# Attention and gated mixing on one core: P times V wholly in float16 passes from pair ten, relu in place in PSUM, row sums turned before their reciprocal

## The chip, the core and the metric

The kernel runs on one NeuronCore of a Trainium2 chip. The core has a matmul engine (TensorE, PE in the profile, with PEld for its weight loads), VectorE (DVE), ScalarE (ACT), GpSimd (POOL) and SyncE (SP), which here issues the DMAs. The metric is the time of one execution on the device in microseconds (us). Three runs of the kernel before gave 939.5, 941.02 and 941.13, median 941.02. A change of less than about 0.2% cannot be told from none.

## The reference

Eight batches, twelve heads, 448 positions, head size 64; everything is float32 at the input and the output.

```python
def rmsnorm(x, g):
    return x / np.sqrt(np.mean(x * x, axis=-1, keepdims=True) + 1e-06) * g
scores = np.matmul(rmsnorm(q, g_q), rmsnorm(k, g_k).transpose(0, 1, 3, 2)) / np.sqrt(64)
attn = np.exp(scores - scores.max(-1, keepdims=True))
attn = attn / (attn.sum(-1, keepdims=True) + 1e-09)
x = np.matmul(attn, v)            # then heads side by side: (8, 448, 768)
h = np.maximum(x @ w_in, 0.0)     # w_in (768, 1024)
# conv: three taps along the sequence, zero at the ends, weights conv_w (3, 1024)
conv = conv_w[0] * h_previous + conv_w[1] * h + conv_w[2] * h_next
out = (h * sigmoid(conv)) @ w_out # w_out (1024, 768)
```

## The kernel before

**Tiles and stages.** Two heads make a pair; there are 48 pairs, six to a batch. A pair's 896 query rows are cut into seven tiles of 128. For a pair the kernel loads q, k and v, squares and sums q and k (L365, L371), forms the inverse root with small steps on the tile `st` (L393 to L408), scales (`apply_rms`), turns k and q into `kT` and `qT`, and multiplies them into seven score tiles (`scores`, L606 and L615). For each tile DVE takes the row maximum (`soft_max`, L619), and ACT forms exp and its row sum (`soft_exp`, L627). The seven sums of a row stand in `rsum`, 128x7.

To multiply P with V, P has to be turned. In pairs 0 to 9 PE turns all seven tiles in float32 (`p_transpose`, L657), ACT or DVE copies them out of PSUM (`p_evac`, tile `PT`), and `pv` (L732) multiplies in float32. In pairs 10 to 47 the first four of the seven tiles take another way: they are split into a float16 high part (`p_hi`) and a float16 rest (`p_lo`), and both are turned by a transposing DMA (`p_turn`, on SP's queue). The other three go on as before. So `pv` has two parts there: 16 instructions in float32 for the 192 columns of each head from the three tiles (L732), and 24 in float16 (L741) for the 256 columns from the four, in three passes: high by high, high by rest of v, rest by high. Both heads' results lie in one PSUM tile, 64 partitions each. For this v is scaled in place by a power of two (`v_scaled`, L705, POOL or DVE), and split into `vp` (`v_hi` on ACT, POOL or DVE; `v_lo` on POOL or DVE).

**Row sums.** `sum_step` adds 1e-9 to `rsum` (L672) and takes the reciprocal (L674), both on DVE; PE turns it to 7x128 (`sum_transpose`, L677, the tile `t_('r'_n`), it is copied out as `rT`, written to memory and read back broadcast over 64 partitions as `rB`. `x_scale` (L748) multiplies pv's result by it, and x is split into two float16 halves.

**The second half.** When a batch has its six pairs, the input stage multiplies x with `w_in` in eight units `fc` of 128 channels, 18 float16 matmuls each (`in_part`, L814, tile `m_('i'_batch_fc`). ACT applies relu out of PSUM into one of two buffers `hbuf` (L824). The middle tap is a scaled copy (`in_conv` 0, L101 on ACT or L103 on DVE), the two outer taps are multiply-adds on DVE (L835), then come tanh on ACT (L841), the gate on DVE (L845), and the split of the gated result into float16 halves (`in_hi`, `in_lo`, L97 and L109). The output stage multiplies these with `w_out` (`out_part`, L884, 24 or more matmuls a tile), copies the result out and stores it.

**Buffers.** PSUM has eight tiles: ring `s` of three for scores, ring `t` of two for transposes, and ring `m` of three, which `pv`, `in_part` and `out_part` share in the order in which they begin. A ring's next tile waits until the tile that many places before has been read for the last time.

**Order of the work.** All steps go into a plan. Each has a due time, from the pair's `base`, offsets in `PH`, and a shift for its name in `SHIFT`; `needs` lists what it waits for, `options` the engines that can do it with a cost, and `PH` an added patience for an engine other than the first. A planner then simulates the engines and writes out one fixed order for each, so that an instruction that waits holds back all that stand behind it on its engine. `SHARED` and `LOCKS` name the steps that, in the planner's model, may not run at the same time on DVE and POOL.

`copy` (L97), `copy_scaled` (L101, L103) and `binary` (L109) are helpers, so many steps share these lines.

Of the kernel before, what the change touches and what calls it, by code (L numbers as in the profile page):

```python
# [19 lines left out]
PH = dict(  # L20
    T=17.282, ti=32.607, si=4.103, so=7.453, hop=0.682, beta=0.029, wi0=-44.74, wi1=135.29,
    wo0=37.16, wo1=179.858, cw=28.289, p_evac=1.569, p_hi=3.998, p_lo=0.384, p_rms=0.085,
    p_v=1.807, p_x=2.279, p_g=2.547, p_relu=3.044, p_cv=0.644, p_qz=2.756, p_ev=0.549, sp=0.066,
    nbulk=3, p_rs=0.015, p_sq=2.22, p_w=4.641, v0=10.619, dg=2, n1=10, q1=10, nf=10, pvs=4,
    p_vs=2.149, p_qh=16.119, p_ql=3.843, p_ph=0.609, p_pl=1.368,
)
PACE = [
    17.594, 18.751, 18.399, 19.788, 14.185, 15.143, 10.221, 13.443, 24.304, 18.98, 20.544,
    19.525,
]  # L30
SHIFT = dict(
    prepare=-39.537, load_g=220.765, make_g=44.125, load_cw=-40.223, make_cw=-61.71,
    load=26.853, convert=189.422, bound=32.819, bound_max=140.72, bound_turn=45.662,
    bound_row=85.601, bound_spread=2.83, scale=25.643, in_factor=265.161, split=128.634,
    rest=-7.056, out_factor=196.209, load_k=256.594, load_q=-7.691, square=166.921,
    square_sum=130.145, rsqrt=76.729, apply_rms=170.731, qk_transpose=55.459, qk_hi=52.477,
    q_middle=-2.488, v_load=240.331, v_bound=-11.069, scores=90.947, soft_max=-2.101,
    soft_exp=75.799, p_transpose=169.491, p_evac=1.057, sum_step=101.401, sum_transpose=184.031,
    sum_evac=42.518, sum_store=11.342, sum_load=0.212, v_scaled=-2.289, pv=113.916,
    x_scale=34.057, x_hi=47.234, x_lo=4.93, v_max=-22.175, v_turn=247.886, v_row=47.937,  # L40
    v_spread=-7.616, v_scale=10.402, qk_lo=-3.699, q_hi=-1.114, q_lo=32.611, q_turn=32.138,
    p_hi=277.959, p_lo=-8.271, p_turn=158.327, v_hi=22.662, v_lo=19.094, moe_scales=-30.954,
    in_part=39.441, in_relu=250.285, in_conv=-0.625, in_tanh=167.33, in_gate=-2.024,
    in_hi=21.395, in_lo=7.763, in_carry=2.204, out_scales=155.356, out_part=185.578,
    out_evac=47.388, out_store=8.134,
# [23 lines left out]
def tile_attention_moe(ctx: ExitStack, tc, q, k, v, g_q, g_k, w_in, conv_w, w_out, out):  # L69
# [41 lines left out]
    def move(e, dst, src):  # L111
# [14 lines left out]
        rB=2, vacc=2, vsc=4, cwb=3, s=3, t=2, m=3, rd=2, rsum=2, rT=2, mx=10, h=2, ph=3, vp=2,  # L126
# [40 lines left out]
    hbuf = [const.tile([P, S + 2], F32, name=f"hbuf{i}") for i in range(BUFS["h"])]  # L167
# [414 lines left out]
    def places(n):  # L582

        if ("PT", n) not in rings.setdefault("PT", Ring(BUFS["PT"])).d:
            new("PT", n, [P, NB * NS * P], F32)
        t, w = old("PT", n), NB * (NS - nd(n)) * P
        return (
            t[:PB, :w].rearrange("p (k q) -> p k q", k=NB),
            t[:, w:].bitcast(F16).rearrange("p (a k q) -> p a k q", a=2, k=NB) if nd(n) else None,
        )  # L590
# [56 lines left out]
    def p_turn(n, j):  # L647
        c = SLOTS[j] if SLOTS[j] < 3 else SLOTS[j] + nd(n) - NS
        nc.sync.dma_start_transpose(
            places(n)[1].rearrange("p a k q -> p (a k) q")[:, :, c * P : (c + 1) * P],  # L650
            old("ph", (n, j)).rearrange("q a k p -> q (a k p)"),
        )
# [7 lines left out]

    def p_evac(n, j):
        c = SLOTS[j] - nd(n) // 2
        copy(
            on["p_evac", n, j], places(n)[0][:, :, c * P : (c + 1) * P],
            old("t", ("p", n, j))[:PB].rearrange("p (k q) -> p k q", k=NB),
        )

    def sum_step(n, i):

        r = old("rsum", n)  # L670
        if i == 0:
            nc.vector.tensor_scalar(r, r, 1e-9, None, op0=ALU.add)  # L672
        else:
            nc.vector.reciprocal(r, r)  # L674
# [6 lines left out]
    def sum_evac(n):  # L681
        copy(on["sum_evac", n], new("rT", n, [NS, P], F32), old("t", ("r", n))[:NS, :P])
# [14 lines left out]
    PV_STEP = PH["pvs"]  # L697
    PV3 = ((0, 0), (0, 1), (1, 0))

    def pvs(n):  # L700
        return (*range(0, NB, PV_STEP), *(range(NB, NB + 3) if nd(n) else ()))
# [14 lines left out]
    def heads(n, k0):  # L716

        wd = nd(n) // 2 * P
        wt = S - wd
        if k0 < NB:  # L720
            return (slice(wd, S), slice(0, wt)), (slice(0, wt), slice(wt, 2 * wt))
        return (slice(0, wd), slice(wt, S)), (slice(0, wd), slice(wd, 2 * wd))

    def pv(n, k0):
        if k0 == 0:
            new("m", ("v", n), [P, 512], F32, psM)
        ps, (out, col) = old("m", ("v", n)), heads(n, k0)
        if k0 < NB:
            v, pt = old("v", n), places(n)[0]
            for k in range(k0, k0 + PV_STEP):  # L730
                for h in range(2):
                    nc.tensor.matmul(  # L732
                        ps[HALF[h], out[h]], v[:, h, k], pt[:, k, col[h]],
# [802 lines left out]
```

## Time and profile before

| | us |
|---|---|
| median of three runs | 941.02 |
| the profiled execution | 939.03 |
| its span, first to last instruction | 937.2 |
| PE busy | 876.9 |
| DVE busy | 747.5 |
| ACT busy | 678.7 |
| POOL busy | 633.9 |

The profile is one execution, recorded by the hardware. "Busy" counts the time in which an engine had an instruction under way; matmuls overlap, so a busy PE need not be at its peak. Windows give busy time by engine in a stretch of the span. The chain that ended last is followed back from the last instruction, at each step to whatever released it. A wait is put down to the releaser that came last. Names of tiles carry the pair or the batch, so `m_('v'_23_5636` is the result of `pv` of pair 23, and a row like `PE t_('r'_14 ... <- DVE rsum` is the transpose of pair 14's sums waiting for DVE. The span falls into a first part of some 180 us with attention alone and the preparing of the weights, a middle in which attention of one batch runs between the input and output stages of an earlier one, and a tail from about 872 us on with only the last batch's input and output stage.

### The profile page before, as it was taken

The page shows a single profiled execution, that of the slowest core. Times are in us where ns is not written, and L with a number is a line of the kernel's source. Part 1 is how long each engine was busy: PE and PEld are TensorE (multiplying, and loading weights), DVE is VectorE, ACT ScalarE, POOL GpSimd, SP SyncE. Part 2 cuts the span into 40 slices and gives each one's busy share as a digit, 9 for nine tenths or more (in the row PEclk, how much of TensorE's full clock was granted, in tenths as well). Part 3 has the DMA queues.
Part 4 walks back from the last instruction along what each step waited for, and adds up shares of the span by engine and source line. Part 5 has one row for each costly group of instructions (what it writes and reads, how often), then busy time and mean ns, then how long its engine had stood idle before and what let it go on. Part 6 is the DMA issues. An engine that isn't in the chain of part 4 may idle for free.

```text
span 937.2 us, 18350 instructions
## 1 busy us (share of the span) xinstructions
PE 876.9 (94%) x6352; PEld 502.8 (54%) x6352; DVE 747.5 (80%) x1308; ACT 678.7 (72%) x1571; POOL 633.9 (68%) x702
## 2 busy tenths in 40 slices
PE   3788899899998999989998999989998999999998
PEld 1344445446654656555655656555654565556555
DVE  6889988898899777897899777897898966991540
ACT  3778879787787876787788876787786877784331
POOL 3483673887888776786877776786877876682120
PEclk9999989999999999999999999999998999999999
DMA  8764452147866768557866679457865777355001
GB/s 195 189 178 131 120 146 66 31 103 162 168 131 122 142 148 174 89 120 153 179 126 119 139 148 185 93 115 152 182 123 91 134 160 135 71 96 116 17 17 51
DMA packets 286572, 117.60 MB, mean 125 GB/s; under 512 B 247744, under 2 KB 282896, under 8 KB 286480
## 3 DMA queue, kind: packets, MB, share of 16 engines
q1 hardware_dynamic: 286480, 116.44, 59.3%
q8 instruction: 50, 0.82, 0.4%
q14 instruction: 42, 0.34, 0.1%
HBM read 56.65 MB, written 11.18 MB: 72 GB/s over the span
## 4 chain that ended last, share of the span: by engine, by line
PE 71%; DVE 19%; ACT 4%; POOL 3%; issue 2%; DMA 1%; SPq 0%; ACTq 0%; DVEq 0%; POOLq 0%
DVE st L371 1%; DVE rsum L672 1%; DVE vacc L534 1%; DVE c_(6_3_10681 L835 1%; DVE wo L216 1%; DVE wo L307 1%; DVE rB L748 1%; PE m_('v'_5_1272 L732 1%; DVE c_(2_4_4782 L835 1%; DVE wi L307 1%; DVE wo L224 1%; PE m_('i'_5_6_9284 L814 1%; DVE carry L860 0%; PE m_('o'_1_0_0_3560 L884 0%; PE m_('o'_5_0_0_9557 L884 0%
## 5 line engine op out<-in xcount | busy, mean ns | idle before, releaser
L814 PEld LDWEIGHTS <-wi 128*128 128x128 f16 x1152 | 113.0, 99 | 97.7 <-issue 7.3
L884 PEld LDWEIGHTS <-gring 128*128 128x128 f16 (+1 forms) x1056 | 102.2, 99 | 58.4 <-issue 5.6
L109 POOL TENSOR_TENSOR sq<-qkf,st 112x512 f32<-112x512 f32 x77 | 88.2, 1159 | 10.6 <-DVE st L393 8.6
L705 POOL TENSOR_SCALAR v<-v,vsc 112x512 f32<-112x512 f32 x37 | 63.1, 1711 | 24.3 <-DVE vsc L206 13.5
L109 POOL TENSOR_TENSOR x<-rB,x 128x448 f16<-128x448 f32 x45 | 49.4, 1098 | 33.2 <-ACT x L97 32.7
L371 DVE TENSOR_REDUCE st<-sq 112x16 f32<-112x1024 f32 x48 | 58.0, 1209 | 6.0 <-ACT sq L365 6.0
L741 PEld LDWEIGHTS <-vp 112*64 112x64 f16 x912 | 49.0, 110 | 7.5 <-issue 4.5
L615 PEld LDWEIGHTS <-qT 64*128 64x128 f16 x684 | 24.3, 94 | 44.8 <-issue 33.7
L365 ACT ACTIVATE sq<-qkf 112x1024 f32<-112x1024 f32 x42 | 44.3, 1056 | 5.0 <-DMA qkf<-in_q_dram 5.0
L109 POOL TENSOR_TENSOR qkf<-sq,qkf 112x512 f16<-112x512 f32 x37 | 46.2, 1249 | 2.2 <-ACT qkf L97 1.9
L109 POOL TENSOR_TENSOR vp<-v,vp 112x512 f16<-112x512 f32 x29 | 35.7, 1232 | 3.1 <-ACT vp L97 1.5
L97 ACT CAST x<-rB 128x448 f16<-128x448 f32 x47 | 26.4, 561 | 11.0 <-DVE rB L748 10.8
L498 POOL COPY qz<-qT 64x128 f16<-64x128 f16 x76 | 31.6, 415 | 3.7 <-DMA qT<-qkf 1.4
L534 DVE TENSOR_REDUCE vacc<-v 112x1 f32<-112x512 f32 x48 | 32.3, 672 | 1.1 <-DMA v<-in_v_dram 0.7
L97 ACT CAST qkf<-sq 112x512 f16<-112x512 f32 x38 | 23.4, 618 | 10.3 <-POOL sq L109 10.3
L672 DVE TENSOR_SCALAR rsum<-rsum 128x7 f32<-128x7 f32 x48 | 27.3, 570 | 3.9 <-ACT e_(47_6_11318 L627 3.4
L884 PEld LDWEIGHTS <-carry 128*64 128x64 f16 x192 | 19.2, 109 | 10.6 <-issue 4.5
L884 PEld LDWEIGHTS <-wi 128*128 128x128 f16 (+1 forms) x192 | 19.4, 101 | 9.7 <-ACT wi L97 0.7
L399 POOL TENSOR_SCALAR st<-st 112x32 f32<-112x32 f32 (+1 forms) x15 | 5.3, 355 | 24.0 <-DVE st L371 23.3
L860 DVE COPY carry<-gring 128x128 f16<-128x128 f16 x32 | 15.1, 472 | 5.7 <-POOL gring L109 5.7
L109 DVE TENSOR_TENSOR sq<-qkf,st 112x512 f32<-112x512 f32 x19 | 18.1, 954 | 1.0 <-POOL st L396 0.9
L494 POOL COPY qz<-qT 64x64 f32<-64x64 f32 x20 | 9.0, 449 | 13.6 <-ACT qT L97 11.4
(3642 smaller groups left out, 3068.7 us busy)
## 6 DMA issues: line engine op xcount, KB each, us to landing
qkf<-in_k_dram SPq DMA_DIRECT2D x48, 224.0 KB
qkf<-in_q_dram SPq DMA_DIRECT2D x48, 224.0 KB
v<-in_v_dram SPq DMA_DIRECT2D x48, 224.0 KB
rB<-rd SPq DMA_DIRECT2D x96, 112.0 KB
wo<-in_moe_w_in_dram SPq DMA_DIRECT2D x12, 512.0 KB
gring<-in_moe_w_out_dram SPq DMA_DIRECT2D x16, 384.0 KB
PT<-ph SPq DMA_TRANSPOSE x152
rd<-rT SPq DMA_DIRECT2D x48, 3.5 KB
```

Of the source, the lines that this page charges most:

```text
L97: (nc.scalar.copy if e == "ACT" else elementwise(e).tensor_copy)(dst, src)
L109: elementwise(e).tensor_tensor(dst, a, b, op=op)
L365: nc.scalar.activation(sq, old("qkf", n), AF.Square)
L371: nc.vector.tensor_reduce(old("st", m)[:, 0, n - m].rearrange("p i s -> p (i s)"), old("sq", n).rearrange("p i h t d -> p (i h t) d"), axi ...
L498: e.tensor_copy(z[HALF[h], :, HALF[h]], old("qT", n)[HALF[h], :, t0 : t0 + 64])
L534: nc.vector.tensor_reduce(old("vacc", b)[:PB, i : i + 1], old("v", n).rearrange("p h t d -> p (h t d)"), axis=AX.X, op=ALU.max, apply_abso ...
L615: nc.tensor.matmul(ps[u][:, :S], lhs, kt[r, w], start=(i == 0), stop=(i == 2))
L672: nc.vector.tensor_scalar(r, r, 1e-9, None, op0=ALU.add)
L705: elementwise(on["v_scaled", n]).tensor_scalar(v, v, old("vsc", n // NP)[:PB, 1:2], None, op0=ALU.mult)
L741: nc.tensor.matmul(ps[HALF[h], out[h]], v[:, w, h, k], pt[:PB, a, k, col[h]], start=(i == 0 and k == 0), stop=(i == 2 and k == NB - 1),)
L814: nc.tensor.matmul(ps[:, :S], wi[:, wl, c, fc * P : (fc + 1) * P], old("x", b * NP + c)[:, xl], start=(i == 0), stop=(i == 3 * NP - 1),)
L884: nc.tensor.matmul(ps[p0 : p0 + m, :NO2], g, wo[:, wl, fc, half * NO2 : (half + 1) * NO2], start=(i == 0), stop=(i == 3 * NFC - 1),)
```

## The change

- From pair ten the three tiles turned by PE are stored as float16 too: `p_evac` writes the high part into `PT`, and a new step `p_low` on DVE subtracts it from the PSUM tile and writes the rest. `pv` is then three float16 passes over all 448 columns of a head, 24 instructions; the float32 part goes away. Pairs 0 to 9 stay as they were.
- In these pairs `v_scaled` goes away: `v_hi` scales while it casts (ACT or DVE, no longer POOL), and `v_lo` multiplies and subtracts in one instruction, on DVE only. The next load into v's buffer waits for `v_lo` instead of `pv`.
- Row sums are turned raw: `sum_transpose` waits for the seven `soft_exp` only; `sum_evac`, on DVE only, adds 1e-9 on the way out of PSUM, and the reciprocal works on `rT`, 7x128.
- relu writes back into the PSUM tile it reads. `in_conv` and `in_gate` read it there, the outer taps on 447 columns, so `hbuf` with its zero columns goes away. The slot of ring `m` is given back at `in_gate`, not at `in_relu`. The first tap's engines are listed with ACT first.
- In the planner `in_conv`, `in_gate`, and `v_lo` and `v_hi` on POOL leave the lists of steps that may not run together. All due times, shifts and patiences have new values, and so the order of all engines is new.

The core of the diff, with the tables of constants left out:

```diff
     def p_evac(n, j):
-        c = SLOTS[j] - nd(n) // 2
         copy(
-            on["p_evac", n, j], places(n)[0][:, :, c * P : (c + 1) * P],
+            on["p_evac", n, j], turned(n, j, 0),
             old("t", ("p", n, j))[:PB].rearrange("p (k q) -> p k q", k=NB),
         )
-    def sum_step(n, i):
-        r = old("rsum", n)
-        if i == 0:
-            nc.vector.tensor_scalar(r, r, 1e-9, None, op0=ALU.add)
-        else:
-            nc.vector.reciprocal(r, r)
+    def p_low(n, j):
+        nc.vector.tensor_tensor(
+            turned(n, j, 1), old("t", ("p", n, j))[:PB].rearrange("p (k q) -> p k q", k=NB),
+            turned(n, j, 0), op=ALU.subtract,
+        )
     def sum_evac(n):
-        copy(on["sum_evac", n], new("rT", n, [NS, P], F32), old("t", ("r", n))[:NS, :P])
+        nc.vector.tensor_scalar(
+            new("rT", n, [NS, P], F32), old("t", ("r", n))[:NS, :P], 1e-9, None, op0=ALU.add
+        )
+    def sum_step(n):
+        nc.vector.reciprocal(old("rT", n), old("rT", n))
...
     def v_hi(n):
-        copy(on["v_hi", n], new("vp", n, [PB, 2, 2, NB, D], F16)[:, 0], old("v", n))
+        copy_scaled(
+            on["v_hi", n], new("vp", n, [PB, 2, 2, NB, D], F16)[:, 0], old("v", n),
+            old("vsc", n // NP)[:PB, 1:2],
+        )
     def v_lo(n):
         vp = old("vp", n)
-        binary(on["v_lo", n], vp[:, 1], old("v", n), vp[:, 0], ALU.subtract)
+        nc.vector.scalar_tensor_tensor(
+            vp[:, 1], old("v", n), old("vsc", n // NP)[:PB, 1:2], vp[:, 0],
+            op0=ALU.mult, op1=ALU.subtract,
+        )
+    def pv(n, i):
+        if i == 0:
             new("m", ("v", n), [P, 512], F32, psM)
+        ps, pt = old("m", ("v", n)), places(n)
         for k in range(NB):
             for h in range(2):
+                if nd(n):
+                    a, w = PV3[i]
+                    lhs, rhs = old("vp", n)[:, w, h, k], pt[:PB, a, k, h * S : (h + 1) * S]
+                else:
+                    lhs, rhs = old("v", n)[:, h, k], pt[:, k, h * S : (h + 1) * S]
                 nc.tensor.matmul(
+                    ps[HALF[h], :S], lhs, rhs, start=(i == 0 and k == 0),
+                    stop=(i == pvs(n)[-1] and k == NB - 1),
                 )
...
     def in_relu(b, fc):
-        ring = rings.setdefault("h", Ring(BUFS["h"]))
-        h = ring.put(("h", (b, fc)), hbuf[ring.count % BUFS["h"]])
-        ps, dst = old("m", ("i", b, fc))[:, :S], h[:, 1 : S + 1]
+        ps = old("m", ("i", b, fc))[:, :S]
         if on["in_relu", b, fc] == "ACT":
-            nc.scalar.activation(dst, ps, AF.Relu, scale=2.0 ** -24)
+            nc.scalar.activation(ps, ps, AF.Relu, scale=2.0 ** -24)
     def in_conv(b, fc, i):
-        h, w = old("h", (b, fc)), old("cwb", b)
+        h, w = old("m", ("i", b, fc)), old("cwb", b)
         if i == 0:
             c = new("c", (b, fc), [P, S], F32)
-            copy_scaled(on["in_conv", b, fc, i], c, h[:, 1 : S + 1], w[:, 1, fc : fc + 1])
+            copy_scaled(on["in_conv", b, fc, i], c, h[:, :S], w[:, 1, fc : fc + 1])
         else:
             c, tap = old("c", (b, fc)), 2 * i - 2
+            dst, src = (slice(1, S), slice(0, S - 1))[:: 1 if i == 1 else -1]
             nc.vector.scalar_tensor_tensor(
-                c, h[:, tap : tap + S], w[:, tap, fc : fc + 1], c, op0=ALU.mult, op1=ALU.add
+                c[:, dst], h[:, src], w[:, tap, fc : fc + 1], c[:, dst], op0=ALU.mult, op1=ALU.add
             )
...
         elif name == "sum_transpose":
-            yield "sum_step", n, 1
+            for j in range(NS):
+                yield "soft_exp", n, j
...
-            in_conv=lambda: [dve(0.675)] if a[2] else [dve(0.45), act(0.66)],
+            in_conv=lambda: [dve(0.675)] if a[2] else [act(0.66), dve(0.62)],
...
-            "in_part": ("in_relu", *a[:2]),
+            "in_part": ("in_gate", *a[:2]),
```

More of the change, by code (lines that the diff above doesn't have):

```diff
@@ L29 @@
-    19.525,
+    18.242, 18.695, 17.598, 20.303, 13.897, 14.369, 11.582, 11.519, 22.84, 20.557, 15.707,
+    20.586,
 ]
 SHIFT = dict(
[L32 to L42, printed above, removed]
@@ L43 @@
-    in_part=39.441, in_relu=250.285, in_conv=-0.625, in_tanh=167.33, in_gate=-2.024,
-    in_hi=21.395, in_lo=7.763, in_carry=2.204, out_scales=155.356, out_part=185.578,
-    out_evac=47.388, out_store=8.134,
+    prepare=-66.106, load_g=331.614, make_g=25.969, load_cw=-61.598, make_cw=-46.515,
+    load=24.101, convert=224.967, bound=45.396, bound_max=205.951, bound_turn=7.69,
+    bound_row=108.526, bound_spread=23.237, scale=3.131, in_factor=269.668, split=208.363,
+    rest=1.758, out_factor=346.937, load_k=169.927, load_q=-8.607, square=235.117,
@@ L46 @@
+    p_hi=290.633, p_lo=-7.497, p_turn=200.607, p_low=0.738, v_hi=93.717, v_lo=80.851,
+    moe_scales=-19.83, in_part=1.8, in_relu=199.52, in_conv=-0.624, in_tanh=295.235,
+    in_gate=-1.263, in_hi=4.981, in_lo=7.824, in_carry=21.742, out_scales=165.779,
+    out_part=266.207, out_evac=65.466, out_store=8.215,
 )
@@ L125, in tile_attention_moe @@
         qkf=3, sq=2, st=2, qT=2, kT=2, qz=2, v=8, sst=6, e=3, PT=2, x=12, c=3,
-        rB=2, vacc=2, vsc=4, cwb=3, s=3, t=2, m=3, rd=2, rsum=2, rT=2, mx=10, h=2, ph=3, vp=2,
+        rB=2, vacc=2, vsc=4, cwb=3, s=3, t=2, m=3, rd=2, rsum=2, rT=2, mx=10, ph=3, vp=2,
     )
@@ L693, in sum_load @@
         )
-    PV_STEP = PH["pvs"]
     PV3 = ((0, 0), (0, 1), (1, 0))
     def pvs(n):
-        return (*range(0, NB, PV_STEP), *(range(NB, NB + 3) if nd(n) else ()))
+        return range(3) if nd(n) else (0,)
     def v_scaled(n):
@@ L778, in plan_attention @@
             at(s + 6.0, sum_load, n, h)
-        at(s - 6.0, v_scaled, n)
-        if nd(n):
+        if not nd(n):
+            at(s - 6.0, v_scaled, n)
+        else:
             at(s - 4.0, v_hi, n)
@@ L1175, in needs @@
             if a[1]:
-                yield "pv", n, pvs(n)[pvs(n).index(a[1]) - 1]
+                yield "pv", n, a[1] - 1
             yield "v_scaled", n
-            if a[1] < NB:
-                for j in range(nd(n), NS):
-                    yield "p_evac", n, j
-            else:
-                yield "v_lo", n
-                for j in range(nd(n)):
-                    yield "p_turn", n, j
+            yield "v_lo", n
+            for j in range(nd(n), NS):
+                yield "p_evac", n, j
+                if a[1] == 2:
+                    yield "p_low", n, j
+            for j in range(nd(n)):
+                yield "p_turn", n, j
         elif name == "x_scale":
@@ L1349, in give @@
             "qk_transpose": ("qk_lo" if ("qk_lo", *a) in steps else "qk_hi", *a),
-            "p_transpose": ("p_evac", *a),
+            "p_transpose": ("p_low" if ("p_low", *a) in steps else "p_evac", *a),
             "sum_transpose": ("sum_evac", *a),
@@ L1493, in tile_attention_moe @@
             free[e] = end - OVER[e]
-            if shared(e, *step):
+            if shared(e, step[0]):
                 port = free[e] - 0.08
```

125 lines of the change are left out of this document (55 added, 70 removed).

## The prediction

> **What bounds the kernel now.** I read the page first for the shares, then the time windows stage by stage, then the chain that ended last, then the waits of the matmul engine, and at the end the durations of the instructions that the change touches.
>
> ```profile
> span 937.2 us, 18350 instructions
> PE 876.9 (94%) x6352; PEld 502.8 (54%) x6352; DVE 747.5 (80%) x1308; ACT 678.7 (72%) x1571; POOL 633.9 (68%) x702
> ```
>
> PE is busy for 94% of the span, DVE for 80%. A mean over unlike stages decides nothing, so here are windows cut along the program. The first fence covers the stretches in which `out_part` runs (first, last and sum of five), the second those in which `in_part` runs (first, fifth and sum of six). The columns are window, length, PE, PEld, DVE, ACT, POOL busy with counts, then the granted clock of PE and the DMA share.
>
> ```profile
> 310.00:361.00 51.00, 51.00 (x429) 30.84 (x429) 37.70 (x81) 36.21 (x85) 38.94 (x41) 1.00 0.77 162
> ...
> 729.00:779.00 50.00, 50.00 (x423) 29.82 (x420) 39.16 (x77) 38.75 (x92) 41.12 (x44) 1.00 0.75 144
> sum 242.00, PE 241.82 PEld 146.13 DVE 193.32 ACT 185.31 POOL 187.49; mean PE 48.37 PEld 29.23 DVE 38.66 ACT 37.06 POOL 37.50
> ```
>
> ```profile
> 255.00:310.00 55.00, 50.71 (x400) 28.84 (x399) 51.85 (x73) 44.14 (x103) 45.61 (x52) 1.00 0.66 130
> ...
> 671.00:729.00 58.00, 53.79 (x400) 30.85 (x398) 51.52 (x71) 43.97 (x100) 45.25 (x52) 0.94 0.64 125
> ...
> sum 339.00, PE 321.78 PEld 184.75 DVE 296.85 ACT 263.42 POOL 256.91; mean PE 53.63 PEld 30.79 DVE 49.48 ACT 43.90 POOL 42.82
> ```
>
> In the output stage PE has no gap (241.82 of 242) and DVE has a fifth free: PE time taken away there is time won. In the input stage PE idles 339 - 321.78 = 17.2 us and DVE is at 88%: there the two engines bound together. The waits of PE say what most of that idle time is:
>
> ```profile
> PE t_('r'_38_9261 L677 <- DVE rsum L674: 4.2, 1, 4.2
> PE t_('r'_26_6280 L677 <- DVE rsum L674: 3.0, 1, 3.0
> PE t_('r'_14_3300 L677 <- DVE rsum L674: 3.0, 1, 3.0
> ```
>
> Three times the transpose of the row sums stands at the head of PE's queue and waits for the reciprocal on DVE, 10.2 us together. What held DVE is the step ahead of it, a 7-element addition (durations in ns: least, median, longest):
>
> ```profile
> L672 DVE TENSOR_SCALAR rsum<-rsum x48: 154/164/5075, 34.9 to 853.5; 128x7 f32<-128x7 f32 x48
> ```
>
> Its median is 164 ns, its longest 5075. The first of the three lies so against POOL's timeline:
>
> ```profile
> 279.05 4.09 DVE L672 TENSOR_SCALAR rsum<-rsum 128x7 f32<-128x7 f32 x1
> ```
>
> ```profile
> 278.60 1.54 POOL L109 TENSOR_TENSOR qkf<-sq,qkf 112x512 f16<-112x512 f32 x1
> ...
> 282.08 1.02 POOL L109 TENSOR_TENSOR gring<-c_(1_3_3152,gring 128x448 f16<-128x448 f32 x1
> ```
>
> POOL runs four subtractions without a gap from 278.60 to 283.10, and DVE's small step ends at 283.14: it was held until POOL paused. A stall has a tail besides, seen in the chain after the third one, where the granted clock of the whole window falls to 0.94:
>
> ```profile
> 707.05 2.24 PE m_('i'_5_5_9234 L814 x6
> 709.30 0.75 PE t_('qk'_40_1_9275 L432 x4
> 710.04 4.70 PE m_('i'_5_6_9284 L814 x18
> 714.74 1.14 PE m_('i'_5_7_9320 L814 x6
> ```
>
> Six matmuls take 2.24 us where later 1.14 do, so eighteen need 3.42 and took 4.70: PE is slow for some microseconds after the gap. These two groups lost 2.4 us.
>
> **The change, part by part.** *P times V.* From pair ten on a pair now takes 16 float32 and 24 float16 instructions; the chain shows two pairs, one unbroken, one cut in three:
>
> ```profile
> 447.93 1.45 PE m_('v'_23_5636 L732 x16
> 449.38 1.31 PE m_('v'_23_5636 L741 x24
> ```
>
> ```profile
> 430.58 1.45 PE m_('v'_22_5390 L732 x16
> 432.03 0.44 PE m_('v'_22_5390 L741 x8
> ...
> 434.16 0.99 PE m_('v'_22_5390 L741 x16
> ```
>
> That is 2.76 us unbroken and 2.88 us cut. A float16 pass of 256 columns takes 0.44 (third line), so one of 448 takes 0.44 x 448/256 = 0.77, three take 2.3, and the turn-over into this shape, 0.99 - 2 x 0.44 = 0.11, makes 2.4 us. The difference is 0.36 to 0.48, I take 0.38; 38 pairs give 14.4 us (13.7 to 18.2), nearly all in stages where PE has no slack. No load, transposing DMA or store is added, so SP's queue carries what it did.
>
> *Row sums turned raw.* The transpose now waits for the last exp on ACT alone. Gone from PE's path are the 10.2 us and the slow tails, at least 2.4 more. DVE's next work held by POOL is later in turn, but PE needs that only through a full ring, so I count 10 (5 to 14). The addition now reads PSUM and the reciprocal follows the transpose: two DVE steps per pair, on the way to x_scale many microseconds later.
>
> *DVE's account.* Removed, from these groups:
>
> ```profile
> L672 DVE TENSOR_SCALAR rsum<-rsum 128x7 f32<-128x7 f32 x48 | 27.3, 570 | 3.9 <-ACT e_(47_6_11318 L627 3.4 <-ACT e_(19_6_4399 L627 0.5
> L674 DVE RECIPROCAL rsum<-rsum 128x7 f32<-128x7 f32 x48 | 9.4, 195 | 0.7
> L705 DVE TENSOR_SCALAR v<-v,vsc 112x512 f32<-112x512 f32 x11 | 12.2, 1131 | 0.0
> L109 DVE TENSOR_TENSOR vp<-v,vp 112x512 f16<-112x512 f32 x9 | 15.1, 1680 | 0.0
> ```
>
> This is 64 us. The taps and gates follow; by line, the 128 taps (L835), then the 64 gates (L845), over the whole span:
>
> ```profile
> 0.00:938.00 938.00, 124.82 (x128) 0.99 0.60 125
> ```
>
> ```profile
> 0.00:938.00 938.00, 53.15 (x64) 0.99 0.60 125
> ```
>
> A tap takes 975 ns in the mean, but one that nothing holds takes 675 (below, both operands in SBUF). With an operand in PSUM the same operation shows 673, and those 38 have a mean of 25.72/38 = 677, so none was held:
>
> ```profile
> L835 DVE SCALAR_TENSOR_TENSOR c_(0_1_1697<-hbuf,cwb,c_(0_1_1697 x2: 671/675/679, 159.3 to 161.8; 128x448 f32<-128x448 f32 x2
> ```
>
> ```profile
> L482 DVE SCALAR_TENSOR_TENSOR kT<-t_('qk'_10_1_1888,G,kT x1: 673/673/673, 181.7 to 181.7; 128x448 f16<-128x448 f32 x1
> ```
>
> ```profile
> 0.00:938.00 938.00, 25.72 (x38) 0.99 0.60 125
> ```
>
> So taps fall by 128 x 0.30 = 38 us and gates by 64 x 0.15 = 10. Here a page speaks against the change. The Trainium skill, "VectorE: DVE Perf Modes", section Rules for kernel authors, advises copying a matmul's result out to SBUF first if many operations will read it, and its table of costs has 120 cycles of fixed cost for a PSUM source against 58. By that, an estimate from its figures, the 192 operations would cost 12 us of DVE more than I count. The rows do not agree, 673 against 675.
>
> Added: 114 subtractions p_low (three per pair, 38 pairs), one operand in PSUM, at 0.68 from the row above: 78 us (0.75, for 512 columns instead of 448, would make 86). Then 38 v_lo, always on DVE and with two SBUF operands: between 0.68 and the 1.68 of the group above, 26 to 64; I take 1.0, nearer the lower end since POOL is relieved: 38. The new addition and reciprocal on 7x128: no row; from below the 0.2 of the 7-element reciprocal, from above 0.67 as for 448 columns; I take 0.3 each, 29 us (19 to 64). Sum: 145 - 64 - 48 = +33 us, DVE 780 of some 920, 85%. It lies beside PE in the output stage; in the input stage a pair adds 3 x 0.68 there but each unit gives 0.75 back, which is about even. The first tap's engine is open, since the planner now asks ACT first.
>
> POOL loses the scaling of v from pair ten, and v_lo:
>
> ```profile
> L705 POOL TENSOR_SCALAR v<-v,vsc 112x512 f32<-112x512 f32 x37 | 63.1, 1711 | 24.3 <-DVE vsc L206 13.5 <-DVE st L401 10.1
> L109 POOL TENSOR_TENSOR vp<-v,vp 112x512 f16<-112x512 f32 x29 | 35.7, 1232 | 3.1 <-ACT vp L97 1.5 <-DVE vsc L802 0.5 <-issue 0.3
> ```
>
> All ten pairs that keep it run on POOL, so 27 x 1.71 + 35.7 = 82 us go. POOL is not on the path; it means fewer holds for DVE.
>
> *relu in place.* This adds a wait. The accumulator in ring m (three slots, shared by in_part, out_part and pv) was free after relu; now it is held until the gate. Unit 4 of batch 3, by its relu and its gate:
>
> ```profile
> L824 ACT ACTIVATE hbuf<-m_('i'_3_4_6121 x1: 556/556/556, 491.5 to 491.5; 128x448 f32<-128x448 f32 x1
> L845 DVE SCALAR_TENSOR_TENSOR c_(3_4_6276<-c_(3_4_6276,hbuf x1: 1167/1167/1167, 500.0 to 500.0; 128x448 f32<-128x448 f32 x1
> ```
>
> That one would be held 9.7 us from relu on. Behind a full ring queue the next in_part and, with PE strictly in order, everything else. The undisturbed chain is relu 0.55, three taps of 0.68, tanh 0.58 (an ACT pass, as relu) and gate 0.62, some 4.4 us with hand-overs. I take 8 us, between the ends, plus 3.4 of accumulation: 11.4. Three slots carry a unit every 3.8 us, two one every 5.7. The units now come every 5.7 us:
>
> ```profile
> L814 PE MATMUL m_('i'_3_0_5845<-x,wi x18: 352/352/353, 460.8 to 464.0; 128*128 128x448 f16 x18
> ...
> L814 PE MATMUL m_('i'_3_7_6340<-x,wi x18: 352/352/353, 501.1 to 506.1; 128*128 128x448 f16 x18
> ```
>
> (506.5 - 460.8) / 8 = 5.7. So the ring only just holds while a pv has the third slot, and I charge 7 us over the seven batches ahead of the last (0 to 28, the upper end in the rivals). In the last batch units follow each other at 3.4 and two later units cover 6.8 of chain: nothing.
>
> *At nothing.* p_low keeps a slot of the two-slot ring t longer, once per tile. Transposes wait for such a slot rarely now:
>
> ```profile
> PE t_('qk'_23_1_5066 L432 <- DVE PT L97: 0.5, 1, 0.5
> ```
>
> With three such tiles in a pair of 17 us other PE work covers it; without that cover it is 0.68 a tile. The casts of v that POOL had go to ACT or DVE and the copy of the turned sums leaves ACT; ACT is at 72% and covers both. v's buffer comes free after v_lo instead of pv, so its load can only start sooner.
>
> *Order.* New due times also move the first 180 us; no row prices that, I leave it at nothing, 6 us either way.
>
> Sum against the profiled execution (937.2 span, 939.0 in all, 1.8 around it): 939.0 - 14.4 - 10 + 7 = 921.6. The median shown, 941.02, lies 2.0 above that execution, so I forecast 923.6, written 924.
>
> **The rivals.** *The ring m runs dry* (slower). Mechanism: gates run as late as in unit 4, DVE being full, so a slot is held 3.4 + 9.7 = 13.1 us and two slots carry one unit per 6.55 us. Against 5.7 that is 0.85 x 56 units = 48 us while pv or an output keeps the third slot. With the third slot away half the time, 24 us, the float16 passes and the raw sums are spent: 939 - 14.4 + 24 = 948.6 and 951 as a median if the stalls on the sums return elsewhere. It decides from about 24 us of waiting, 0.43 per unit. The Trainium skill, "PSUM — Partial Sum Buffer", section Summary: rules for kernel authors, says to evacuate promptly because the space is tight, and this change does the opposite. Against it: the order is new and can put the chain first. Chance 0.13.
>
> *DVE becomes the bound of the input stage.* Then what PE saves there (339 of the 581 us in the two fences, 8.4 of the 14.4) and the stalls on the sums are void, and of DVE's 33 us, 19 fall there, which its own idle time (339 - 296.85 = 42) takes up in part, say half: 939 - 6 + 9 = 942, 944 as a median, between no change and slower. For it stands the 88%, against it that taps and gates lose their holds just there. Chance 0.10.
>
> *The holds were the whole trouble.* With taps, gates and sums off the shared SBUF access all 17.2 us of input-stage idle time and 4 us of slow tails go, no slot is missed: 939 - 14.4 - 21 = 903.6, 906 as a median. Chance 0.15.
>
> That the float16 passes do not do what they say, because a pass is bound by its weight loads, is excluded by the 0.44 for eight matmuls with eight loads at half the columns.
>
> **How the numbers follow.** My forecast has 0.62. Its own range is 910 to 936: PV 13.7 to 18.2, sums 5 to 14, ring 0 to 16, first stage 6 either way, not all at one end. The range reaches to the middle of the other cases: 906 to 943. A change within 0.2% (1.9 us) cannot be told from none here. Faster: 0.62 + 0.15 = 0.77. Same: 0.04 of the DVE case and 0.01 of the ring, 0.05. Slower: the rest of these two, 0.18.
>
> **What would show it.** Right: PV groups of 24 at 2.4 us, no wait of `t_('r'` on DVE, taps at 0.68, PE gapless in the output stage. Wrong: PE waits at an in_part or a pv for a gate (ring m), at scores for soft_max (DVE), or holds of several microseconds on v_lo with PE waiting behind them; the sum then fails at the 7, at the even account of DVE, or at the 10.

## The result, and the profile after

The changed kernel takes 912.95 us (median of 4 runs, 910.32 to 913.88); the kernel before, beside it, 940.26 (938.26 to 941.13). The ratio is 0.9708, with a 95% interval of 0.9681 to 0.9735: 27.3 us faster, where 17 were forecast. The profiled execution took 912.52 us, 1.8 of them outside the span. Its page begins so:

```profile
span 910.7 us, 17210 instructions
PE 860.4 (94%) x5744; PEld 463.3 (51%) x5744; DVE 764.4 (84%) x1386; ACT 692.6 (76%) x1558; POOL 563.0 (62%) x673
```

PE's busy time fell by 16.5 us and its idle time by 10.0 (60.3 to 50.3). So more than a third of the gain is time in which PE waited. Where it came from is read from the start of the first matmul of `in_part` in each batch (us from the span's start; the last column is the stretch from that of the last batch to the end):

| kernel | batch 0 | batch 1 | batch 3 | batch 7 | to the end |
|---|---|---|---|---|---|
| before | 141.0 | 247.7 | 460.8 | 872.1 | 65.1 |
| after | 145.2 | 252.3 | 453.3 | 843.8 | 66.9 |

The changed kernel is still 4.6 us *late* at batch 1, 7.5 ahead at batch 3, and gains 20.8 us in the 24 pairs between batch 3 and batch 7. That stretch as one time window, before and after (window, length, PE, PEld, DVE, ACT, POOL busy with counts, granted clock, DMA share):

```profile
460.00:872.00 412.00, 401.28 (x3148) 237.34 (x3144) 327.10 (x553) 307.98 (x711) 300.77 (x323) 0.99 0.66 129
```

```profile
453.00:844.00 391.00, 389.06 (x2778) 211.43 (x2777) 341.39 (x609) 313.14 (x704) 248.03 (x312) 1.00 0.71 137
```

PE's busy time falls by 12.2 us (0.51 per pair) and its idle time from 10.7 to 1.9. After, PE has hardly a gap left there, while DVE is busier than before by 14 us and POOL less by 53.

The lines that answer to those of before. P times V, from the chain of a window, is one group of 24:

```profile
279.69 2.39 PE m_('v'_13_3188 L738 x24
296.37 2.39 PE m_('v'_14_3419 L738 x24
```

On DVE the taps (L833), the gates (L843) and the new `p_low` (L672) by line over the whole span, and from the page the rows of `v_lo` and of the new reciprocal (busy, mean ns, idle before):

```profile
0.00:911.00 911.00, 86.50 (x128) 0.99 0.62 129
```

```profile
0.00:911.00 911.00, 39.33 (x64) 0.99 0.62 129
```

```profile
0.00:911.00 911.00, 77.46 (x114) 0.99 0.62 129
```

```profile
L722 DVE SCALAR_TENSOR_TENSOR vp<-v,vsc,vp 112x512 f16<-112x512 f32 x38 | 37.1, 976 | 0.1
L688 DVE RECIPROCAL rT<-rT 7x128 f32<-7x128 f32 x48 | 44.9, 935 | 0.7
```

A tap has gone from 975 to 676 ns and a gate from 830 to 615. `p_low` takes 0.68 and `v_lo` 0.98, as forecast (0.68 and 1.0). The reciprocal on 7x128 takes 0.935 us, three times the 0.3 assumed. The waits of PE (us in total, times, longest):

```profile
PE t_('qk'_0_0_151 L432 <- POOL sq L110: 13.9, 1, 13.9
PE t_('p'_4_4_969 L656 <- ACT PT L98: 4.1, 1, 4.1
PE m_('o'_7_1_0_11460 L882 <- DVE c_(7_7_11443 L843: 2.6, 1, 2.6
...
PE t_('r'_9_2101 L678 <- DVE PT L98: 1.0, 1, 1.0
```

The three waits of 4.2, 3.0 and 3.0 us for the row sums are gone; the longest of a `t_('r'` is 1.0. The first line is there before as well (14.3 us). Only one wait of size has a gate behind it, in the last batch, 2.6 us. How long a slot of ring m is held shows in unit 4 of batch 3, its relu and its gate:

```profile
L821 ACT ACTIVATE m_('i'_3_4_5990<-m_('i'_3_4_5990 x1: 525/525/525, 481.6 to 481.6; 128x448 f32<-128x448 f32 x1
```

```profile
L843 DVE SCALAR_TENSOR_TENSOR c_(3_4_6120<-c_(3_4_6120,m_('i'_3_4_5990 x1: 620/620/620, 486.3 to 486.3; 128x448 f32<-128x448 f32 x1
```

From 481.6 to 486.9 it is 5.3 us, where from relu to the end of the gate the same unit took 9.7 before. Over the 56 units of the first seven batches this time is 5.7 us in the mean, 8.7 before.

### The profile page after: what moved, and what is told of

Same layout as the page of the kernel before. It is cut to its first block, busy times and chain, and to the rows that moved or that the text cites. A ratio compares the mean times of both kernels' runs of the same rounds, so it can differ in the third digit from the quotient of the medians.

```text
span 910.7 us, 17210 instructions
## 1 busy us (share of the span) xinstructions
PE 860.4 (94%) x5744; PEld 463.3 (51%) x5744; DVE 764.4 (84%) x1386; ACT 692.6 (76%) x1558; POOL 563.0 (62%) x673
## 4 chain that ended last, share of the span: by engine, by line
PE 66%; DVE 23%; ACT 5%; issue 2%; DMA 2%; SPq 1%; POOL 0%; ACTq 0%; DVEq 0%; POOLq 0%
DVE st L371 2%; DVE rT L688 1%; DVE PT L672 1%; DMA v<-in_v_dram 1%; DVE rB L745 1%; DVE wo L220 1%; DVE wo L224 1%; DVE wo L216 1%; DVE carry L858 1%; DVE vacc L534 1%; DVE PT L98 1%; PE m_('o'_7_0_0_11432 L882 1%; ACT PT L98 1%; DVE vp L722 1%; DVE kT L482 1%
## 5 line engine op out<-in xcount | busy, mean ns | idle before, releaser
L110 POOL TENSOR_TENSOR sq<-qkf,st 112x512 f32<-112x512 f32 x92 | 102.2, 1120 | 7.9 <-DVE st L393 3.1
L738 PEld LDWEIGHTS <-vp 112*64 112x64 f16 x912 | 47.9, 110 | 42.0 <-issue 10.7
L110 POOL TENSOR_TENSOR x<-rB,x 128x448 f16<-128x448 f32 x44 | 47.0, 1067 | 22.2 <-ACT x L98 21.8
L688 DVE RECIPROCAL rT<-rT 7x128 f32<-7x128 f32 x48 | 44.9, 935 | 0.7
L110 POOL TENSOR_TENSOR qkf<-sq,qkf 112x512 f16<-112x512 f32 x32 | 38.4, 1201 | 0.5 <-ACT qkf L98 0.3
L722 DVE SCALAR_TENSOR_TENSOR vp<-v,vsc,vp 112x512 f16<-112x512 f32 x38 | 37.1, 976 | 0.1
L399 POOL TENSOR_SCALAR st<-st 112x32 f32<-112x32 f32 (+1 forms) x17 | 4.2, 246 | 46.2 <-DVE st L371 46.1
L498 POOL COPY qz<-qT 64x128 f16<-64x128 f16 x76 | 24.1, 317 | 3.8 <-PE s_(44_5_10334 L614 1.2
L102 ACT ACTIVATE vp<-v,vsc 112x512 f16<-112x512 f32 x31 | 22.3, 719 | 0.2 <-DVE vsc L206 0.2
L395 POOL TENSOR_SCALAR st<-st 112x32 f32<-112x32 f32 (+1 forms) x34 | 12.3, 361 | 12.5 <-DVE st L408 7.0
L710 POOL TENSOR_SCALAR v<-v,vsc 112x512 f32<-112x512 f32 x9 | 18.1, 2017 | 1.1 <-DVE st L408 0.9
L406 POOL TENSOR_TENSOR st<-st 112x32 f32<-112x32 f32 (+1 forms) x30 | 8.9, 295 | 14.0 <-DVE st L401 11.6
```

The costliest lines, as they stand in the source:

```text
L110: elementwise(e).tensor_tensor(dst, a, b, op=op)
L498: e.tensor_copy(z[HALF[h], :, HALF[h]], old("qT", n)[HALF[h], :, t0 : t0 + 64])
L688: nc.vector.reciprocal(old("rT", n), old("rT", n))
L722: nc.vector.scalar_tensor_tensor(vp[:, 1], old("v", n), old("vsc", n // NP)[:PB, 1:2], vp[:, 0], op0=ALU.mult, op1=ALU.subtract,)
L738: nc.tensor.matmul(ps[HALF[h], :S], lhs, rhs, start=(i == 0 and k == 0), stop=(i == pvs(n)[-1] and k == NB - 1),)
```

## The experiments

The change has four parts: P times V in float16, raw row sums, relu in place, and new due times. In the expectations P is the prediction's own account, H says that the holds between DVE and POOL were the trouble, O that the new order did it; ring and DVE theories are those of the rivals. "Own order" means that the listed order of work is that of the kernel it was made from, "replanned" that the planner made a new one; a replanned run thus changes the order as well as the part. A ratio is to the kernel before, run on the same chip.

**The parts under the old due times.** The changed code with the constants (`PH`, `PACE`, `SHIFT`) of before:

```diff
-    sw=0.0, f_pl=0.008, f_ql=0.208, f_lo=0.049, f_rms=0.0, f_sq=0.497, T=17.282, ti=32.607,
+    T=17.282, ti=32.607, si=4.103, so=7.453, hop=0.682, beta=0.029, wi0=-44.74, wi1=135.29,
...
-                    sw = PH["sw"]
+                    sw = PH.get("sw", 0.0)
```

> All four parts of the change, but the due times, shifts and patiences of the kernel before (what is new among the constants is nothing); the planner makes the order anew from them. Theory P (the parts themselves bring the 27 us): 913 to 925 us. Theory O (the newly searched due times bring most of it, the parts little): 932 to 945. Theory H (the parts bring it, but only through the holds between DVE and POOL): as P, and without the waits of PE for the row sums.

918.62 us, ratio 0.9762 (0.9739 to 0.9785). The parts bring 22 us, the new due times 5.

**The new due times alone.** The code before with the constants of after (the same edit the other way round).

> The kernel before with the new due times, shifts and patiences, order made anew, none of the four parts. Theory P: 935 to 950 us, PE waits for the reciprocal of the row sums again. Theory O: 912 to 925.

963.64 us, ratio 1.0239 (1.0195 to 1.0283). O falls: these due times cost the old code 22 us. They bring a gain only together with the new parts.

**Raw sums alone**, in the code before, own order:

```diff
     def sum_step(n, i):
-        r = old("rsum", n)
...
+        pass
     def sum_evac(n):
-        copy(on["sum_evac", n], new("rT", n, [NS, P], F32), old("t", ("r", n))[:NS, :P])
+        r = new("rT", n, [NS, P], F32)
+        nc.vector.tensor_scalar(r, old("t", ("r", n))[:NS, :P], 1e-9, None, op0=ALU.add)
+        nc.vector.reciprocal(r, r)
```

> The kernel before in its own order, with one part alone: sums turned raw, addition and reciprocal on DVE at the place where the copy out of PSUM was. Theories P and H: the three stalls of 3.0 to 4.2 us and the slow stretch behind them go, 10 to 14 us less, 926 to 930 us. Rival (DVE bound): the reciprocal on 7x128 takes 0.93 us instead of 0.2, 36 us more on DVE, no gain or up to 10 us slower, 940 to 950. Theory O: within 2 us of 940.

953.05 us, ratio 1.0131 (1.0107 to 1.0155): slower, against P and H, and by slightly more than the DVE rival had. The waits on `t_('r'` are gone, but the transposes of later tiles now wait for an exp that came late:

```profile
PE t_('p'_39_4_9330 L657 <- ACT e_(39_4_9320 L627: 3.8, 1, 3.8
...
PE t_('p'_15_4_3400 L657 <- ACT e_(15_4_3385 L627: 2.1, 1, 2.1
PE t_('p'_27_4_6370 L657 <- ACT e_(27_4_6360 L627: 2.1, 1, 2.1
```

All such waits of a `t_('p'` sum to 31 us against 12 before. DVE's busy time rose by 19 us, to 766.7. The chain ahead of the longest of them (start, us, what) shows where the hold went:

```profile
716.62 3.40 DVE c_(5_4_9212 L103
...
721.43 0.94 DVE rT L680
...
727.30 0.54 DVE sst_(39_4_9312 L619
727.87 0.73 ACT e_(39_4_9320 L627 x2
```

A middle tap takes 3.40 us on DVE, where the 32 of the kernel before take 0.57 in the mean, and POOL runs subtractions without a gap until 719.76, just ahead of its end at 720.02. Then come the new reciprocal, the row maximum and the late exp. The addition can no longer be held ahead of PE's transpose, but another step of DVE is.

**P times V in float16 alone**, in the code before, own order, with `p_low` straight after each copy:

```diff
     def p_evac(n, j):
...
+        copy(on["p_evac", n, j], t[:PB, 0, :, x], ps)
+        nc.vector.tensor_tensor(t[:PB, 1, :, x], ps, t[:PB, 0, :, x], op=ALU.subtract)
     def pv(n, k0):
...
+            if nd(n):
+                return
```

> The kernel before in its own order, with one part alone: P times V in three float16 passes from pair ten and the 114 subtractions p_low on DVE right behind each copy; scaling and split of v, sums and relu as before. Theory P: PE time is won, 38 pairs by 0.4 us, 14 to 18 us less, 922 to 926 us. Rival (DVE bound): 77 us of new work on DVE take it back, 938 to 950. Theory H: in between, since no hold goes, 930 to 938.

982.27 us, ratio 1.0433 (1.0402 to 1.0464): 41 us slower. The order was not made for it, so it was tried again with an order of its own and with v scaled in its cast (old due times):

```diff
+            if nd(n):
+                at(s + j * d + 6.0, p_low, n, j)
...
+        copy_scaled(
+            on["v_hi", n], new("vp", n, [PB, 2, 2, NB, D], F16)[:, 0], old("v", n),
+            old("vsc", n // NP)[:PB, 1:2],
+        )
```

> The kernel before with one part alone, P times V in float16 passes with p_low and v scaled in its cast, its own due times, the order made anew by the planner, which knows the new steps. If the 41 us that the same part cost in the old order came from an order that did not know p_low: 922 to 932 us. If DVE has no room for 77 us more while taps, gates and sums are held: 940 to 965.

966.99 us, ratio 1.0284 (1.0244 to 1.0325). P times V alone costs 27 us even in a fresh order. Its window from batch 3 to batch 7:

```profile
471.00:901.00 430.00, 400.90 (x2774) 215.30 (x2773) 351.14 (x618) 312.34 (x721) 270.74 (x309) 0.98 0.62 124
```

PE has as few matmuls as in the changed kernel, yet idles 29.1 us of 430, and its busy time does not fall either (400.90, with the granted clock at 0.98). The 77 us of `p_low` lie on a DVE whose taps are still held (117 us for the 128). It is not that DVE is full: it is busy for 82% of this window, and for 87% in the changed kernel.

**relu in place alone**, code before, old due times, replanned:

```diff
     def in_relu(b, fc):
-        ring = rings.setdefault("h", Ring(BUFS["h"]))
-        h = ring.put(("h", (b, fc)), hbuf[ring.count % BUFS["h"]])
-        ps, dst = old("m", ("i", b, fc))[:, :S], h[:, 1 : S + 1]
+        ps = old("m", ("i", b, fc))[:, :S]
+        dst = ps
...
-            "in_part": ("in_relu", *a[:2]),
+            "in_part": ("in_gate", *a[:2]),
```

> The kernel before with one part alone, relu in place in PSUM with taps and gate reading there, its own due times, the order made anew by the planner, which now gives the accumulator's slot back at the gate. Theory H2 (the holds on taps and gates are the largest item, and relu in place pays for the new work on DVE): taps at 0.68 us, 45 to 50 us less on DVE, 915 to 930 us. Theory ring (slots held until the gate cost as much): 938 to 950, with PE waiting at in_part or pv. Theory T (only all parts together gain): within 4 us of 941.

921.06 us, ratio 0.9795 (0.9766 to 0.9824): 19 us faster by the ratio, with no matmul changed. From its page, then its taps (L835):

```profile
PE 872.1 (95%) x6352; PEld 502.7 (55%) x6352; DVE 682.3 (74%) x1304; ACT 679.8 (74%) x1573; POOL 597.3 (65%) x708
```

```profile
0.00:919.00 919.00, 86.66 (x128) 0.99 0.60 128
```

DVE loses 65 us (taps 38, gates 14, the additions to the row sums 12) and POOL 37 with nearly the same work: both had been waiting for each other inside their instructions. In the kernel before 52 of the 128 taps take over 0.85 us, and 47 of these end 0.5 us after the end of an instruction of POOL; so do all 23 such gates. With relu in place no tap and no gate takes over 0.85. All traces bear this out: taking for every instruction what it took beyond the shortest of the same operation, tiles and shape in the same trace (an estimate of the holds), the six runs in which relu writes to SBUF sum to 160 to 189 us on DVE and 82 to 92 on POOL, the eight with relu in place to 107 to 136 and 37 to 55.

The row sums, left as they were, are held less too:

```profile
L672 DVE TENSOR_SCALAR rsum<-rsum x48: 155/168/2006, 35.1 to 831.3; 128x7 f32<-128x7 f32 x48
```

The longest addition is 2.0 us instead of 5.1, and the waits of PE for `t_('r'` sum to 1.8 us instead of 12.7. But the order is new as well. The additions of two other replanned runs, P times V alone (above, relu to SBUF) and the sums ahead of the transpose (below, relu in place):

```profile
L688 DVE TENSOR_SCALAR rsum<-rsum x48: 148/161/1025, 35.4 to 882.3; 128x7 f32<-128x7 f32 x48
```

```profile
L688 DVE TENSOR_SCALAR rsum<-rsum x48: 152/171/3451, 34.4 to 839.1; 128x7 f32<-128x7 f32 x48
```

The waits for `t_('r'` are 16.8 us in the first and 6.8 in the second. So the stalls that the prediction gave to the raw sums can go without raw sums, but how much of that is relu in place and how much the order was not separated.

**relu out to SBUF in the changed kernel**, own order, two buffers:

```diff
     def in_relu(b, fc):
-        ps = old("m", ("i", b, fc))[:, :S]
+        ring = rings.setdefault("h", Ring(2))
+        h = ring.put(("h", (b, fc)), hbuf[ring.count % 2])
+        ps, dst = old("m", ("i", b, fc))[:, :S], h[:, 1 : S + 1]
     def in_conv(b, fc, i):
-        h, w = old("m", ("i", b, fc)), old("cwb", b)
+        h, w = old("h", (b, fc)), old("cwb", b)
```

> The changed kernel in its own order, one part undone: relu writes to two buffers in SBUF, taps and gate read there, the accumulator's slot comes free after relu. Theory H: taps and gates are held by POOL again, 40 to 50 us more on DVE, 6 to 15 us more in all, 919 to 928 us. Theory ring (the slot held until the gate costs what the prediction charged, 7 us): 5 to 8 us less, 905 to 908. Theory O or a DVE with room: within 3 us of 913.

974.06 us, ratio 1.0319 (1.026 to 1.0377): 58 us slower than the changed kernel by the ratios. The ring theory, which had this one faster, falls; the size is beyond what H expected. From its page, two of its waits, and the chain ahead of the first of these waits (start, us, what):

```profile
PE 881.7 (91%) x5744; PEld 472.2 (49%) x5744; DVE 816.3 (84%) x1386; ACT 698.0 (72%) x1558; POOL 610.4 (63%) x677
```

```profile
PE t_('p'_39_4_9171 L657 <- ACT e_(39_4_9157 L627: 6.7, 1, 6.7
PE t_('p'_27_4_6272 L657 <- ACT e_(27_4_6258 L627: 6.7, 1, 6.7
```

```profile
737.57 0.80 DVE c_(5_5_9094 L835
738.39 1.33 DVE c_(5_5_9094 L835
739.73 1.23 DVE vp L723
741.10 0.62 DVE c_(5_5_9094 L845
741.75 0.56 ACT wi L98
742.31 0.70 ACT e_(39_4_9157 L627 x2
743.06 1.10 PE t_('p'_39_4_9171 L657 x4
744.16 2.24 PE m_('i'_5_7_9120 L814 x6
```

DVE is 52 us longer and POOL 47, and the taps are at 128 us for 128 again. PE idles 41 us more, and with the same matmuls it is busy 21 us more, at a granted clock of 0.96 instead of 0.99. It stands 6.7 us at a transpose whose exp on ACT comes behind the cast of a gated result (`in_hi`, here into a place in the tile `wi`), and that behind a row of DVE steps with a tap of 1.33 us in it; afterwards the slow tail is there too, 2.24 us for six matmuls. The two buffers are not what costs: all the waits at a relu in this run are for `in_part`, and none is for the gate that frees a buffer. But this order was planned for taps that POOL does not hold, so a part of the 58 us may be the order.

**The sums ahead of the transpose, in the changed kernel**, own order:

```diff
     def sum_transpose(n):
+        r = old("rsum", n)
+        nc.vector.tensor_scalar(r, r, 1e-9, None, op0=ALU.add)
+        nc.vector.reciprocal(r, r)
         nc.tensor.transpose(
```

> The changed kernel in its own order, one part undone: addition and reciprocal on DVE on the 128x7 sums ahead of the transpose, at the transpose's place in the order, and a DVE copy of the turned sums behind it. Theories P and H: the 7-element addition is held by POOL again and PE waits behind it, 8 to 15 us more, 921 to 928 us. Rival (the reciprocal on 7x128, 0.93 us against 0.2, costs as much as the holds did): within 4 us of 913. Theory O: within 2 us of 913.

949.69 us, ratio 1.0086 (1.0059 to 1.0114), 36 us above the changed kernel by the ratios, more than any theory had. The waits and the addition:

```profile
PE t_('r'_8_1816 L681 <- DVE rsum L680: 3.8, 1, 3.8
PE t_('r'_14_3278 L681 <- DVE rsum L680: 2.7, 1, 2.7
PE t_('r'_9_2112 L681 <- DVE rsum L680: 2.7, 1, 2.7
```

```profile
L679 DVE TENSOR_SCALAR rsum<-rsum x48: 155/274/1976, 32.7 to 870.5; 128x7 f32<-128x7 f32 x48
```

The waits on `t_('r'` sum to 46 us. Two runs split this number. In the first only the reciprocal stands ahead of the transpose; it leaves out adding 1e-9:

```diff
     def sum_transpose(n):
+        r = old("rsum", n)
+        nc.vector.reciprocal(r, r)
...
-        nc.vector.tensor_scalar(
-            new("rT", n, [NS, P], F32), old("t", ("r", n))[:NS, :P], 1e-9, None, op0=ALU.add
-        )
+        nc.vector.tensor_copy(new("rT", n, [NS, P], F32), old("t", ("r", n))[:NS, :P])
```

> The changed kernel in its own order; the reciprocal is taken on the 128x7 sums ahead of the transpose and the addition of 1e-9 is left out (each sum holds the exp of 0 and so is at least 1, where float32 does not show 1e-9); the turned sums are copied by DVE. DVE has 48 x 0.74 = 36 us less than in the changed kernel. If the addition was what POOL held and the reciprocal is not held: 905 to 912 us. If every DVE step ahead of the transpose stalls PE: 918 to 928. If DVE has room anyway: within 2 us of 913.

925.11 us, ratio 0.9806 (0.9747 to 0.9864), on the chip of the run before and 25 us below it.

```profile
L679 DVE RECIPROCAL rsum<-rsum x48: 183/190/196, 33.1 to 840.8; 128x7 f32<-128x7 f32 x48
```

The reciprocal is never held (183 to 196 ns), and still the waits on `t_('r'` sum to 25 us: at this place in the order it stands behind other work of DVE. In the second the sums stand ahead of the transpose, but the planner places them (new due times):

```diff
+        for i in range(2):
+            at(s + 2.0 + 0.3 * i, sum_step, n, i)
         at(s + 3.0, sum_transpose, n)
         at(s + 3.5, sum_evac, n)
-        at(s + 3.7, sum_step, n)
```

> The changed kernel with its due times and one part undone, sums added to and inverted ahead of the transpose, the order made anew by the planner, which knows it. If the 37 us that this cost in the given order were a matter of order: 911 to 919 us. If the wait of PE on DVE and the hold of the addition are the price: 922 to 940.

926.37 us, ratio 0.9848 (0.9817 to 0.9879). So raw sums are worth 13 us in the changed kernel, under due times that were chosen with raw sums in it; the other 22 of the 36 were the place.

**Four matmuls more per pair in P times V** of the changed kernel, whose sums are overwritten; from the group of 24, 4/24 of (2.39 - 0.11), 0.38 us:

```diff
+        if nd(n) and i == 0:
+            for k in range(2):
+                for h in range(2):
+                    nc.tensor.matmul(
+                        ps[HALF[h], :S], old("vp", n)[:, 0, h, k],
+                        pt[:PB, 0, k, h * S : (h + 1) * S], start=(k == 0), stop=(k == 1),
+                    )
```

> The changed kernel in its own order with four more float16 matmuls of 448 columns per pair from pair ten (their sum is overwritten by the passes that follow), 0.37 us of PE each pair, about what the change took away. Theory P: PE bounds, 38 x 0.37 = 14 us more, 927 us. Rival (DVE bounds by now, at 84%): 0 to 6 us more, 913 to 919.

923.75 us, ratio 0.9784 (0.9736 to 0.9833). For 38 x 0.38 = 14 us put on PE the time rises by 7 us by the ratios and 11 by the medians: half to three quarters. The interval is too wide for more than that PE time is worth something there, but not all of its face value.

**A version that goes further**: the reciprocal straight out of PSUM in place of the addition, one DVE step fewer per pair; it leaves out adding 1e-9:

```diff
     def sum_evac(n):
-        nc.vector.tensor_scalar(
-            new("rT", n, [NS, P], F32), old("t", ("r", n))[:NS, :P], 1e-9, None, op0=ALU.add
-        )
+        nc.vector.reciprocal(new("rT", n, [NS, P], F32), old("t", ("r", n))[:NS, :P])
     def sum_step(n):
-        nc.vector.reciprocal(old("rT", n), old("rT", n))
+        pass
```

> The changed kernel in its own order, the reciprocal taken straight out of PSUM in the place of the addition, and no second step (1e-9 is left out; each sum is at least 1). DVE has 48 x 0.27 = 13 us less and PE waits for nothing new. If DVE still bounds the first 220 us, where ten such steps lie: 908 to 912 us. If not: within 2 us of 913.

906.96 us, ratio 0.9645 (0.9622 to 0.9669), 6 us below the changed kernel: the fastest of all. The reciprocal takes as long from PSUM:

```profile
0.00:906.00 906.00, 44.98 (x48) 0.99 0.62 130
```

What goes is the addition, 13 us of DVE (48 x 0.27).

## Why the prediction was right, and where it was not

The direction and the range held, and the time landed between the forecast and the rival of the holds. The attribution did not hold, and that is the larger lesson: taken alone, in the runs made, the two terms counted as gains cost time and the one counted as a loss gains it. That their sum still came within 11 us was in part luck. (The lower end of the range, 906, is the whole time of the rival of the holds; the middle between it and 910 would be 908. Both hold the measured time.) The combinations that were run, as ratios; where the due times are called old or new, the run is replanned:

| relu in place | P times V float16 | sums raw | due times | ratio |
|---|---|---|---|---|
| yes | no | no | old | 0.9795 |
| no | yes | no | old | 1.0284 |
| no | yes | no | own order of before | 1.0433 |
| no | no | yes | own order of before | 1.0131 |
| yes | yes | no | new | 0.9848 |
| yes | yes | no | own order of after | 1.0086 |
| no | yes | yes | own order of after | 1.0319 |
| yes | yes | yes | old | 0.9762 |
| yes | yes | yes | new | 0.9708 |
| no | no | no | new | 1.0239 |

Alone, relu in place, P times V and raw sums are worth -19, +27 and +12 us of 941 by these ratios; their sum would be +20, together under the old due times they are -22. (The +12 is from the own order; raw sums alone were not replanned, and a part of that may be their place in it.) They are not terms of a sum. Two of the three take DVE time and one gives it; with relu in place and under the same due times, the other two together cost nothing (0.9762 against 0.9795).

*The step that failed: relu in place, +7 for ring m.* It was counted as a wait added, its gain as DVE time that "is about even" with `p_low`. In the runs it is the part that carries the change: -19 us alone, and 58 lost when it is undone. What failed is the step from a held slot to a waiting PE. The slots are held about as long as assumed where relu in place stands alone (from relu to the end of the gate 7.1 us in the mean of the first seven batches, against the 8 taken), and in the run of all parts under the old due times unit 4 of batch 3 is held 9.8 us. Still no `in_part` or `pv` of the changed kernel waits for a gate, nor of the run with relu in place alone, and under the old due times such waits sum to 1.1 us. (2.6 us fall in the last batch, at an `out_part`, where nothing was counted.) What the term left out is that held instructions of DVE reach PE through the strict order of work, wherever they stand. The mechanism stood in the rival of the holds, with a chance of 0.15; that was too little.

The Trainium skill, "SBUF — State Buffer", section Who interferes with whom, says that a DVE instruction with two SBUF inputs contends with a GpSimd instruction that reads SBUF, and one with at most one SBUF input does not unless it is in a 2-port mode. The taps agree: 0.68 us with an operand in PSUM, 1.0 with both in SBUF. The rule against this change that the prediction weighed, in the Trainium skill, "VectorE: DVE Perf Modes", section Rules for kernel authors (it names two ways, to read PSUM or to copy the result out first for many operations), is decided by the measurement here: with POOL busy beside DVE, relu into SBUF costs 19 us in the kernel before and up to 58 in the changed one.

*The row sums, -10.* The waits were read rightly and their size was right (12.7 us of waits before, 1.6 after). That the addition is held by POOL was read rightly too: each of the 13 in the kernel before that took over 0.5 us ends 0.02 to 0.03 us after the end of an instruction of POOL. But these waits also go without raw sums (1.8 us with relu in place alone, replanned), and raw sums alone do not save them, since the hold then stands at another step of DVE. What raw sums bring once relu is in place is 13 us, with two DVE steps taken from between the last exp and PE's transpose.

*P times V, -14.4.* The duration was right (2.39 against 2.4). That 38 x 0.38 would come off the time was not: alone it costs 27 us. `p_low` was put "at nothing" as other work of PE would cover it; on a DVE whose steps are still held PE idles instead (29.1 us of the 430 shown). With relu in place but sums ahead of the transpose it is still no gain (0.9848 against 0.9795 without it, though under other due times); with raw sums and the new due times it is 8 us better. Between batch 3 and batch 7, relu alone takes 402.5 us, the changed kernel under the old due times 402.2, under the new ones 390.5; the new due times without the parts take 412.1. So the 12 us there need the parts and the new order together. How they divide between PE time and order stays open.

*DVE's account.* Forecast 780, the page has 764. `p_low` (78, measured 77.5), `v_lo` (38, 37.1) and taps with gates (-48, -52) were right. The addition and reciprocal were put at 29 and take 13.0 + 44.9 = 58, mis-sized by the reciprocal, within the bounds given. By the groups of the two traces, most of what made up for it is work that the new order gives to other engines: on DVE the scaling of q and k (`sq`) falls from 18.1 to 3.6 us, the middle taps from 18.1 to 6.7, a step on the weights (`wi`, `wo`) from 15.4 to 4.6 and the output copies from 8.6 to none. DVE does not bound the middle after: PE idles 1.9 of 391 us there with DVE at 87%.

*Order, 0 within 6.* The input stage of the first batch starts 4.2 us late. The reciprocals add DVE time there (0.935 instead of 0.195), and that is enough to account for it: with raw sums alone in the old order it starts at 145.1, in the changed kernel at 145.2, without the addition at 142.3, and with the reciprocal on 128x7 and no addition at 141.0, as before. But with the sums ahead of the transpose, replanned, it starts at 143.3, so a share of the order is not excluded. The new due times as a whole bring 5 us.

## What to carry to other kernels

When two engines hold each other inside their instructions, the busy time of both is too long, and the stalls appear elsewhere, at whatever stands behind the held instruction; look at the least and the longest duration of a small instruction before pricing the place where the wait shows. Parts of a change that draw on one engine cannot be priced one by one: the part that frees it can take away the cost of the part that loads it. And work "at nothing" needs its cover checked in the kernel as it will be then: float16 passes that save PE 0.38 us per pair cost 27 us while DVE's steps were held.

## What was not expected of the hardware

The reciprocal's time goes with the elements per partition: 0.19 us for 128x7 (183 to 196 ns), 0.935 for 7x128, the same from SBUF and from PSUM. That is (935 - 190) / 121 = 6.2 ns an element; the addition on 7x128 takes 0.27. And the reciprocal on 128x7 was not held once in 48, nor behind the addition in the seven other runs that have it (182 to 203 ns), while the addition on the same tile in the same place was held up to 1.98 us, and up to 5.08 in the kernel before.
